# Strided 768 KB transfers issued from ScalarE's DMA queue in a two-part attention and long-convolution kernel

## The chip, the cores and the metric

The kernel runs on one core of one Trainium2 chip. Time is device time in microseconds (us) from one launch; the number that counts is the median of several runs. A profile of one execution comes with it: for each engine what ran when, what it waited for, and every packet of the DMA engines. TensorE (PE) multiplies matrices, VectorE (DVE), ScalarE (ACT) and GpSimd (POOL) do elementwise work, SyncE (SP) only issues DMAs. ScalarE may issue DMAs as well, from its own queue; in the page the queue of SyncE is q1 and that of ScalarE q10. The issues themselves are listed under SPq and ACTq, and are not counted as busy time.

## The reference

Two computations with no data in common write the left and the right half of one output (2048 x 1152, bfloat16).

Part A is attention with a compressive memory: 32 heads of 18 channels, 2048 positions in four segments of 512. Within a segment it is causal softmax attention; beside it, each segment reads a memory of all earlier segments; a gate per head mixes the two; a last product with `wo` follows.

```python
for s in range(N):
    logits = jnp.einsum('bhqd,bhkd->bhqk', qs, ks) * scale + mask
    a_dot = jnp.einsum('bhqk,bhkd->bhqd', _softmax(logits, axis=-1), vs)
    pq = phi(qs)
    a_mem = einsum(pq, M) / (einsum(pq, z) + 1e-06)
    outs.append(g * a_mem + (1.0 - g) * a_dot)
    pk = phi(ks)
    M, z = M + einsum(pk, vs), z + sum(pk)
return o @ wo
```

Part B is a gated long convolution over 576 channels: a four-tap convolution of `k`, times `v`, then a convolution with a filter of 2048 taps (`ssm_k`) by Fourier transforms, then a product with `q`.

```python
kv = k_shift * v
y = irfft(rfft(kv_pad) * rfft(kf_pad))[:S] + kv * ssm_D
return q * y
```

## The kernel before

**Tiling.** Part A goes over 4 segments and, in each, over 4 groups of heads `p`. The projections `proj_qk` and `proj_v` (L548, L607) read the transposed input `xT`; q and k go to a scratch tensor in DRAM (`store_rows`, L529) and come back with the channels of one head group on the right partitions (`load_heads`, L598, the tile `qk`). `scores` and `scores2` multiply them (L686), ScalarE takes the exponential into `PT` (L692), GpSimd masks (L698), `av` multiplies with V (L737). Numerators and denominators go through DRAM as well: `norm` stores `ou` (L752), `weights` fetches the denominators `cs` (L775) and stores their reciprocals (L790), `dense` fetches both as `nt` and `rt` (L811, L813), and `out_proj` multiplies with `wo` (L833) and stores (L839). `phik` fetches k once more, transposed by the DMA (L635); `load_x` does so with the next segment's input (L522).

Part B goes over three groups of 192 channels. `kv_prep` loads `k` and `v` transposed by the DMA (L1056), convolves four taps on TensorE (L1066), multiplies (L1070) and stores `kv_scratch` (L1074). `load_xs` (L1082) brings either the filter `ssm_k` or `kv_scratch` into the tile `xs` with 64 elements (128 bytes) to a piece: 6144 pieces, 768 KB. It is called six times, three for the filter and three for `kv_scratch`. `f1` (L1097) and `f2` (L1115) are the forward transform, `kloop` the products `Y` (L1152 to L1159), `inverse` (L1134) and `finish` (L1176, L1184) the way back. `last` loads `q_sb` (L1230), 768 KB in pieces of 384 bytes, and stores the result from the same tile (L1234). `begin` adds the small tensor `Dt` to `xs` (L1199) before `f1` can start; `Dt` and the taps `sk_bf` are loaded at L1042 to L1046.

**What sets the order.** The program is recorded first, as operations with their reads and writes. `Graph.plan` then lays them out one by one with its own cost for each: among the operations that can start within 0.3 us of the earliest on an engine it takes the one with the lowest priority number. An operation with alternatives (an eviction may run on VectorE or ScalarE) goes where the planned end is earlier, with a bias. `rank` gives priorities from the place in the recording, shifted by the table SHIFT; BIAS shifts the choice of engine, JOIN says where two TensorE operations are planned with their buffers together. Each engine then executes its list strictly in that order; so does each DMA queue. A DMA is an operation on the list of the engine that issues it; nearly all are on SyncE's, while ScalarE issues only the second half of the first input and most of `wk`.

In the planner a DMA occupies its issuer for a fixed time, then 16 modelled engines for a time that follows from number and size of its pieces; it lands a receipt time later. There are eight completion lanes that all DMAs of both issuers take in turn: a DMA waits until the one eight before it has landed.

**Where the planner puts fillers.** `gaps` finds planned holes of TensorE with much work around them, and puts matmuls on the identity there (L1359) that compute nothing of use.

**Names at the start.** `load0` is the first input and the weights `wq`, `wk` (L419, L420); `load1` is `wv` and the last columns of `wk`; `late_consts` with the label `late` copies `wo` within DRAM (L436), reloads it in another order (L441, L442), and loads `beta`. `tab` are the sine tables: two activations of 128 x 2048 (IS, IC) and smaller ones, on ScalarE, which needs another activation table for sines than for exponentials. `FI` is made from `FR` by a DMA (L991, L992).

Of the kernel before, what the change touches and what calls it, by code (L numbers as in the profile page):

```python
# [36 lines left out]
PEQ, ACTQ, DVEQ, POOLQ, SPQ = "PE", "ACT", "DVE", "POOL", "SP"  # L37
# [75 lines left out]
class Graph:  # L113
    SEM, DRAIN, SWITCH, MATE = 0.07, 0.2, 0.1, 0.03
    START, RECEIPT, LANES = 0.5, 1.3, 8
# [48 lines left out]
    def plan(self):  # L164
        free = {e: 0.0 for e in (PEQ, ACTQ, DVEQ, POOLQ, SPQ)}
        busy = dict(free)
        queue, lands = [0.0] * 16, [0.0] * self.LANES
# [3 lines left out]
        while left:  # L171
            best = {}
            for o in cand:
# [13 lines left out]
                for eng, us, emit in o.alts:  # L187
                    st = max(free[eng], t0)
                    for d in o.deps:
                        st = max(st, d.land + self.sem(d, eng))  # L190
                    best.setdefault(eng, []).append((st, o, us, emit, sl))
# [27 lines left out]
            if o.parts:  # L219

                e, one = st, us / len(o.parts)
                for n, share, k, ahead in o.parts:
                    e = max(e, lands[-self.LANES]) + one
                    for q in range(k):
                        queue[q] = max(queue[q], e - ahead + self.START) + share
                    lands.append(max(queue[0:k]) + self.RECEIPT)
                o.end, o.land = e, max(lands[-len(o.parts):])
# [113 lines left out]
class Part:  # L341
# [24 lines left out]
    def dma(self, parts, fn, r=(), w=(), us=0.4, ahead=0.0, by=(SPQ,)):  # L366

        nc = self.nc
        us *= len(parts)
        q = {SPQ: nc.sync, ACTQ: nc.scalar, POOLQ: nc.gpsimd}  # L370
        share = [(n, n * (8.0 + b / 27.0) * 1e-3 / k, k, ahead) for n, b, k in parts]
        return self.G.op([(e, us + (0.0 if e == SPQ else 0.15 * len(parts)), lambda e=e: fn(q[e])) for e in by], r, w, share)
# [528 lines left out]
class PartB(Part):  # L901
# [176 lines left out]
    def load_xs(self, src2d, g, keys):  # L1078
# [4 lines left out]
            "(c e) (a n) -> (e a) c n", e=4, a=KA)), r=keys, w=[xs])  # L1083
# [142 lines left out]
    def last(self, g):  # L1226
# [3 lines left out]
        self.dma([(2048, 384, 16)], lambda dq: dq.dma_start(out=q[:], in_=self.q_view[:, :, ch0:ch0 + GB]), w=[q])  # L1230
        for qq in range(0, QS, 8 * FD):
# [3 lines left out]
                 r=[(q, qq) for qq in range(0, QS, 8 * FD)])  # L1235
# [28 lines left out]
def rank(ops, a, b, shift):  # L1264
# [9 lines left out]
    'tab': 0.013, ('xs', 'in_B_ssm_k_dram', 0): 0.022, 'load0': -2, 'tr0': -1, ('qk', 0, 'first'): -1.5, ('qk', 0, 0): -1,  # L1274
    ('qk', 0, 5): -1, ('qk', 0, 6): -0.183, ('qk', 0, 4): -0.88, ('v', 0, 1): -0.168, ('x', 1): -0.088, ('qk', 1, 0): -0.572,
    ('sc', 0, 0, 0): 0.484, ('pk', 0): -0.042, ('sc', 0, 0, 1): 0.597, ('s2', 0, 1): -0.916, ('sc', 0, 1, 0): -0.046,
    ('sc', 0, 1, 1): 0.017, ('mem', 0): 0.054, ('s2', 0, 2): 0.007, ('no', 0, 1): 0.012, ('qk', 1, 1): -0.001,
    ('sc', 0, 2, 0): -0.002, ('av', 0, 2, 0): -0.222, ('s2', 0, 3): -0.013, ('qk', 1, 6): -0.152, ('sc', 0, 3, 1): 0.013,
    ('x', 2): -0.042, ('s2', 1, 0): -1.089, ('qk', 2, 0): 0.02, ('pk', 1): 0.555, ('v', 2, 0): 0.031, ('de', 0, 4): 0.327,
    ('sc', 1, 0, 1): -0.003, ('av', 1, 0, 0): -0.69, ('s2', 1, 1): -0.08, ('qk', 2, 5): -0.017, ('sc', 1, 1, 0): -0.011,  # L1280
    ('v', 2, 1): -0.009, ('sc', 1, 1, 1): -0.013, ('av', 1, 1, 0): -0.01, ('out', 0, 0): 0.015, ('qk', 2, 1): 0.02,
    ('sc', 1, 2, 0): -0.003, ('v', 2, 2): -0.006, ('s2', 1, 3): 0.006, ('qk', 2, 6): 0.001, ('av', 1, 3, 0): -0.302,
    ('no', 1, 3): -0.457, ('pk', 2): -0.017, ('de', 1, 0): 0.181, ('av', 2, 0, 1): -0.115, ('out', 1, 0): -0.327,
    ('v', 3, 2): 0.029, ('sc', 2, 2, 1): 0.014, ('out', 1, 1): 0.005, ('s2', 2, 3): 0.011, ('qk', 3, 6): 0.358,
    ('sc', 2, 3, 0): 0.003, ('v', 3, 3): 0.005, ('qk', 3, 4): -0.014, ('av', 2, 3, 1): 0.012, ('de', 2, 0): 1.659,
    ('de', 2, 3): -0.039, ('de', 2, 4): 0.397, ('sc', 3, 1, 0): 0.011, ('sc', 3, 1, 1): 0.01, ('s2', 3, 2): 0.029,
    ('sc', 3, 2, 0): 0.015, ('sc', 3, 2, 1): 0.029, ('out', 2, 2): 0.022, ('s2', 3, 3): 0.041, ('sc', 3, 3, 0): 0.04,
    ('sc', 3, 3, 1): 0.04, ('av', 3, 3, 0): 0.33, ('out', 2, 3): 0.03, ('de', 3, 0): 0.474, ('de', 3, 1): 0.369,
    ('de', 3, 2): -0.147, ('de', 3, 3): -0.427, ('de', 3, 4): -0.816, ('f1', 'A_h', 5, 8): -1.107, ('f1', 'A_h', 5, 16): -0.575,
    ('f1', 'A_h', 5, 24): 0.106, ('f1', 'A_h', 5, 32): 0.765, ('kv', 0, 9): -0.772, ('kv', 0, 1): 0.645, ('kv', 0, 3): -0.493,  # L1290
    ('kv', 1, 9): -0.286, ('kv', 1, 3): -0.791, ('xs', 'kv_scratch_69', 0): -1.316, ('f1', 'A_kv', 8, 0): -0.437,
    ('f1', 'A_kv', 8, 8): -1.241, ('f1', 'A_kv', 8, 16): -0.041, ('f1', 'A_kv', 8, 24): -0.654, ('f1', 'A_kv', 8, 32): -0.895,
    ('f1', 'A_kv', 8, 40): -0.691, ('row', 0, 0): -0.143, ('kv', 2, 0): -0.191, ('row', 0, 8): -1.15, ('y', 0, 8): -1.492,
    ('kv', 2, 1): -0.06, ('y', 0, 1): 1.118, ('row', 0, 9): 0.009, ('row', 0, 2): 0.003, ('inv', 8, 1): 0.005,
    ('kv', 2, 3): 0.004, ('row', 0, 10): 0.004, ('y', 0, 10): 0.184, ('inv', 8, 2): 0.021, ('f1', 'A_h', 10, 0): 0.032,
    ('row', 0, 11): 0.035, ('y', 0, 4): 0.464, ('f1', 'A_h', 10, 8): -0.018, ('row', 0, 12): 0.033,
    ('f1', 'A_h', 10, 16): 0.033, ('y', 0, 5): 0.438, ('inv', 8, 4): -0.118, ('row', 0, 13): 0.015, ('row', 0, 6): -0.192,
    ('f1', 'A_h', 10, 32): -0.381, ('row', 0, 14): 0.005, ('row', 0, 7): -0.109, ('row', 0, 15): 0.02,
    ('f1', 'A_kv', 11, 8): -0.007, ('fin', 8, 16): -0.325, ('fin', 8, 24): 0.02, ('f1', 'A_kv', 11, 24): 0.011,
    ('fin', 8, 32): 0.018, ('f1', 'A_kv', 11, 32): 0.018, ('f1', 'A_kv', 11, 40): -0.008, ('kv', 3, 1): -0.005,  # L1300
    ('row', 1, 1): -0.008, ('y', 1, 1): 0.115, ('kv', 3, 3): 0.04, ('row', 1, 10): 0.01, ('kv', 4, 9): 0.238,
    ('y', 1, 4): 0.131, ('inv', 11, 3): 0.01, ('kv', 4, 1): -0.668, ('kv', 4, 2): 0.096, ('y', 1, 13): -0.573,
    ('row', 1, 6): 0.011, ('inv', 11, 5): 0.003, ('f1', 'A_h', 14, 0): -0.486, ('row', 1, 14): 0.005,
    ('f1', 'A_h', 14, 8): -0.006, ('row', 1, 15): 0.002, ('f1', 'A_h', 14, 16): -0.018, ('f1', 'A_h', 14, 24): -0.022,
    ('f1', 'A_h', 14, 32): -0.025, ('f1', 'A_h', 14, 40): -0.062, ('f1', 'A_kv', 15, 0): -0.025, ('f1', 'A_kv', 15, 8): -0.029,
    ('f1', 'A_kv', 15, 16): -0.032, ('f1', 'A_kv', 15, 24): -0.008, ('f1', 'A_kv', 15, 32): 0.01, ('row', 2, 8): -0.001,
    ('row', 2, 9): 0.005, ('inv', 15, 1): 0.036, ('y', 2, 10): -0.075, ('y', 2, 3): 0.113, ('row', 2, 11): 0.019,
    ('row', 2, 4): 0.014, ('y', 2, 4): -0.471, ('inv', 15, 3): -0.508, ('row', 2, 12): -0.093, ('row', 2, 5): 0.344,
    ('y', 2, 5): 0.047, ('y', 2, 13): 0.644, ('row', 2, 6): 0.421, ('y', 2, 14): 0.452, ('row', 2, 7): -0.091,
    ('fin', 11, 0): 0.443, ('fin', 11, 16): -0.052, ('fin', 11, 24): -0.347, ('fin', 11, 40): -0.361, ('fin', 15, 24): -0.732,  # L1310
    ('fin', 15, 32): 0.277,
}
BIAS = {
    None: 0.3, 'tr0': 0, ('qk', 0, 0): 0, ('av', 0, 2, 1): 0, ('av', 1, 0, 0): 0.6, ('out', 0, 2): 1, ('av', 1, 2, 1): 1,
    ('v', 2, 3): -1.5, ('av', 1, 3, 0): 0, ('qk', 2, 4): -0.3, ('qk', 3, 0): -0.6, ('out', 1, 1): 3, ('out', 1, 3): -1.5,
    ('av', 3, 1, 0): 0.6, ('av', 3, 1, 1): -0.3, ('av', 3, 2, 0): 1.5, ('out', 2, 1): -1.5, ('out', 2, 2): -1.5,
    ('out', 3, 1): 0, ('f1', 'A_h', 5, 0): -0.6, ('y', 0, 0): 1, ('y', 0, 8): 1, ('y', 0, 1): 1, ('y', 0, 9): 1, ('y', 0, 2): 1,
    ('y', 0, 10): 1, ('y', 0, 3): 1, ('y', 0, 11): 1, ('row', 0, 4): -0.6, ('y', 0, 4): 3, ('y', 0, 12): 1, ('y', 0, 5): 1,
    ('y', 0, 13): 1, ('row', 0, 6): 1.5, ('y', 0, 6): -0.6, ('y', 0, 14): 1, ('row', 0, 7): -0.3, ('y', 0, 7): 1,
    ('f1', 'A_h', 10, 40): 3, ('y', 0, 15): 1, ('row', 1, 0): 0, ('y', 1, 0): 0, ('row', 1, 8): -1.5, ('y', 1, 8): 1,  # L1320
    ('y', 1, 1): 1, ('inv', 11, 0): 1.5, ('y', 1, 9): 1, ('y', 1, 2): 1, ('y', 1, 10): -0.3, ('y', 1, 3): 1, ('y', 1, 11): 1,
    ('y', 1, 4): 1, ('y', 1, 12): 1, ('y', 1, 5): 1, ('y', 1, 13): 1, ('row', 1, 6): -0.6, ('y', 1, 6): 1, ('y', 1, 7): 3,
# [70 lines left out]
```

## Time and profile before

| | |
|---|---|
| median of 13 runs | 353.01 us |
| lowest, highest | 349.58, 355.36 us |
| profiled execution | 352.95 us |
| its span, first to last instruction | 351.0 us |
| mean granted TensorE clock in it | 0.92 |

All times in what follows are inside the span of the profiled execution unless a run is named; 1.95 us lie around it. The page divides the span into 40 slices of 8.8 us; each digit is a busy share in tenths.

```profile
PE   4992999679885788779998888899897679977995
ACT  4571775767886389779796688776787876968850
DMA  8976969895476754591799668775977283252365
```

The fourth slice, from 26 to 35 us, is TensorE's emptiest. A timeline has one row for each instruction (or run of like ones): start, length, engine, line, operation, destination and source. SPq is an instruction of SyncE's queue: its length is the time for which it held the queue, and not the time of the transfer. In the chain of waits the work that ended last is followed backwards; "DMA x<-y" there is the time from issue to landing.

### The profile page before, as it was taken

What the parts mean: (1) busy time and instruction counts of PE and PEld (TensorE: products, weight loads), DVE (VectorE), ACT (ScalarE), POOL (GpSimd) and SP (SyncE); (2) the same over time, 40 slices, a digit from 0 to 9 for tenths busy, and PEclk for the clock granted to TensorE, in tenths of its full rate; (3) what the DMA queues carried; (4) which work ended last, traced back from release to release, by engine and by line L of the source; (5) the groups of instructions that cost most, each with busy time, mean ns of one, the idle gap of its engine ahead of it and who ended that gap; (6) DMA issues with size and microseconds to landing.
All of it is one profiled execution on the core that took longest, in us unless ns stands there. A gap on an engine that the chain in (4) does not pass through costs nothing.

```text
span 351.0 us, 9299 instructions
## 1 busy us (share of the span) xinstructions
PE 292.5 (83%) x3776; PEld 164.0 (47%) x3776; DVE 269.3 (77%) x390; ACT 248.0 (71%) x279; POOL 191.1 (54%) x262
## 2 busy tenths in 40 slices
PE   4992999679885788779998888899897679977995
PEld 3452545434453253556653344445454335544673
DVE  8953776576776289988976698898889795969993
ACT  4571775767886389779796688776787876968850
POOL 7723121167366359644246574795766368678710
PEclk9998899996999599999999699999999855989998
DMA  8976969895476754591799668775977283252365
GB/s 249 209 173 151 205 134 193 187 226 140 149 153 134 160 106 131 153 211 29 191 203 213 148 175 232 187 186 162 198 219 203 50 220 99 69 156 67 108 151 157
DMA packets 120369, 56.91 MB, mean 162 GB/s; under 512 B 93096, under 2 KB 113096, under 8 KB 120328
## 3 DMA queue, kind: packets, MB, share of 16 engines
q1 hardware_dynamic: 119448, 55.45, 65.6%
q10 hardware_dynamic: 880, 0.88, 0.8%
q8 instruction: 29, 0.48, 0.6%
q14 instruction: 12, 0.10, 0.1%
HBM read 25.66 MB, written 21.80 MB: 135 GB/s over the span
## 4 chain that ended last, share of the span: by engine, by line
PE 43%; DVE 17%; DMA 17%; ACT 9%; issue 7%; SPq 4%; POOL 2%; DVEq 0%; ACTq 0%; POOLq 0%
PE banks L548 8%; ACT PT L692 6%; DMA qk<-a_qk_scratch 6%; PE banks L833 5%; PE banks L686 5%; PE banks L1066 4%; PE banks L1134 3%; PE banks L607 3%; PE banks L737 3%; PE banks L1097 3%; DVE ou L363 3%; PE banks L1115 3%; DMA kv<-in_B_k_dram 2%; DMA rt<-a_r_scratch 2%; DVE nt L819 2%
## 5 line engine op out<-in xcount | busy, mean ns | idle before, releaser
L692 ACT ACTIVATE PT<-banks 128x1024 bf16<-128x1024 f32 x160 | 155.6, 1030 | 38.6 <-PE banks L686 30.9
L698 POOL TENSOR_SCALAR_AFFINE_SELECT PT<-PT 128x512 bf16<-128x512 bf16 (+1 forms) x112 | 83.3, 757 | 99.2 <-ACT PT L692 96.0
L686 PE MATMUL banks<-qk 18*128 18x512 bf16 (+3 forms) x512 | 54.1, 318 | 18.3 <-DMA qk<-a_qk_scratch 7.4
L548 PE MATMUL banks<-xT,wqk 128*128 128x512 bf16 x180 | 47.7, 407 | 2.2 <-DMA xT<-in_A_x_dram 0.7
L1152 POOL TENSOR_TENSOR Y<-HX 128x768 bf16<-128x768 bf16 x19 | 33.4, 1762 | 18.3 <-DVE HX L363 9.2
L686 PEld LDWEIGHTS <-qk 18*128 18x128 bf16 x512 | 16.2, 94 | 48.0 <-issue 31.6
L363 DVE CAST HX<-banks 128x768 bf16<-128x768 f32 x27 | 25.7, 956 | 11.1 <-PE banks L1115 9.4
L1158 POOL TENSOR_TENSOR Y<-Y 128x192 bf16<-128x192 bf16 x40 | 25.8, 645 | 10.8 <-DVE Y L1152 10.0
L363 DVE CAST A_kv<-banks 128x768 bf16<-128x768 f32 (+1 forms) x26 | 27.3, 1064 | 5.5 <-PE banks L1134 2.8
L1097 PE MATMUL banks<-W1bd,xs 128*64 128x128 bf16 x576 | 22.5, 231 | 10.0 <-DVE xs L1199 6.7
L363 DVE CAST ou<-banks 128x1024 bf16<-128x1024 f32 (+1 forms) x23 | 24.8, 1079 | 5.0 <-PE banks L737 3.2
L548 PEld LDWEIGHTS <-wqk 128*128 128x128 bf16 x180 | 16.9, 102 | 24.8 <-issue 10.4
L737 PE MATMUL banks<-PT,V 128*32 128x256 bf16 (+3 forms) x512 | 25.3, 318 | 2.4 <-ACT PT L692 0.8
L1097 PEld LDWEIGHTS <-xs 128*64 128x64 bf16 x576 | 19.0, 117 | 15.3 <-issue 7.9
L1159 POOL TENSOR_TENSOR Y<-Y 128x192 bf16<-128x192 bf16 x40 | 26.0, 650 | 0.0
L833 PE MATMUL banks<-wo_sb,o_sb 128*128 128x288 bf16 x160 | 24.6, 312 | 1.6 <-DVE o_sb L820 1.0
L1066 PE MATMUL banks<-kv,dg 128*128 128x512 bf16 x80 | 20.1, 387 | 5.1 <-DMA kv<-in_B_k_dram 4.4
L1134 PE MATMUL banks<-Y,IC 64*128 64x192 bf16 x192 | 22.2, 260 | 1.7 <-DVE V L363 0.6
L607 PE MATMUL banks<-wv,xT 128*128 128x288 bf16 x160 | 23.1, 297 | 0.4 <-ACT HX L364 0.4
L364 ACT CAST HX<-banks 128x768 bf16<-128x768 f32 x21 | 16.8, 805 | 5.6 <-PE banks L1115 5.3
L819 DVE TENSOR_TENSOR nt<-nt,rt 128x1024 bf16<-128x1024 bf16 (+1 forms) x15 | 18.4, 1228 | 3.1 <-DMA rt<-a_r_scratch 3.1
L833 PEld LDWEIGHTS <-o_sb 128*128 128x128 bf16 x160 | 16.4, 106 | 8.9 <-issue 1.8
(146 smaller groups left out, 535.9 us busy)
## 6 DMA issues: line engine op xcount, KB each, us to landing
a_o_scratch<-ou SPq DMA_DIRECT2D x12, 512.0 KB
qk<-a_qk_scratch SPq DMA_DIRECT2D x48, 108.0 KB
a_qk_scratch<-q SPq DMA_DIRECT2D x32, 128.0 KB
nt<-a_o_scratch SPq DMA_DIRECT2D x12, 256.0 KB
rt<-a_r_scratch SPq DMA_DIRECT2D x12, 256.0 KB
xs<-in_B_ssm_k_dram SPq DMA_DIRECT2D x3, 768.0 KB
xs<-kv_scratch SPq DMA_DIRECT2D x3, 768.0 KB
q_sb<-in_B_q_dram SPq DMA_DIRECT2D x3, 768.0 KB
```

The source lines that it names most:

```text
L363: return self.G.op([(DVEQ, dve_us(n, 0.53 if bf else 1.042), lambda: nc.vector.tensor_copy(out=out(), in_=in_())), (ACTQ, act_us(n), lambd ...
L548: nc.tensor.matmul(pq[:], lhsT=self.wqk[:, t, 128 * m:128 * m + P], rhs=xT[:, t, :], start=(t == 0), stop=(t == 4))
L607: nc.tensor.matmul(out, lhsT=xT[:, t, P * tt:P * tt + P], rhs=self.wv[:, t, 288 * h:288 * h + 288], start=(t == 0), stop=(t == 4))
L686: nc.tensor.matmul(ps[:, j - j0, off:off + n], lhsT=qk[r, 2 + u, P * kt:P * kt + P], rhs=qk[r, u, P * kt:L], start=True, stop=True, tile_p ...
L692: self.act(act_us(512 * SE), lambda a=a, ps=ps, j=j, j0=j0: nc.scalar.activation(out=a(dst), in_=ps[:, j - j0:j - j0 + SE, :], func=ACT.Ex ...
L698: self.pool(0.2 + n * 0.13, lambda: nc.gpsimd.affine_select(out=ap(), in_=ap(), compare_op=ALU.is_ge, fill=0.0, base=0, pattern=[[0, n], [ ...
L737: nc.tensor.matmul(po[32 * j:32 * j + 32, 0, P * kt:L], lhsT=V[:, kt, 19 * h:19 * h + 32], rhs=rhs, start=(kt == 0), stop=(kt == 3), tile_ ...
L833: nc.tensor.matmul(ps[:, i, 0:288], lhsT=o[:, t, P * qt:P * qt + P], rhs=self.wo[:, t, 288 * h:288 * h + 288], start=(t == 0), stop=(t == ...
L1066: self.pe(pe_us(*[512] * 4 * w), lambda c=c, ps=ps: [nc.tensor.matmul(ps[:, 512 * h:512 * h + 512], lhsT=dg[:, i, :], rhs=t[:, 0, KPAD + 5 ...
L1097: nc.tensor.matmul(ps[64 * h:64 * h + 64, u, :], lhsT=xs[:, c0 + u, :], rhs=self.W1[:, h].rearrange("p e k -> p (e k)"), start=True, stop= ...
L1134: nc.tensor.matmul(ap(b)[:, o, :], lhsT=tab[q, r + 8 * h, :], rhs=Ys[h][q, n, :], start=(h == n == 0), stop=(h == n == 1), tile_position=( ...
L1152: eng.tensor_tensor(out=Y[:].rearrange("p (x h) c -> p x h c", x=2), in0=HX[:, 1, :].rearrange("p (x c) -> p x c", x=2).unsqueeze(2).to_br ...
```

## The change

It has five parts.

1. `load_xs` (all six loads of `xs`) and the load of `q_sb` in `last` are issued by ScalarE (`by=(ACTQ,)`). The stores of the result may be issued by either; the planner chose ScalarE for the last of the three and SyncE for two.
2. The planner has a set of 16 modelled engines for each of the two queues. A transfer on one is lengthened by what the other still has to do, up to its own time, and lengthens the other by as much.
3. It knows a limited room: after a transfer, the next DMA of the same queue may start only when all but the last 80 pieces of each ring (RING) are done.
4. No transfer is planned to run before 2.2 us (FIRST), and bytes are costed at 23 instead of 27 a nanosecond.
5. SHIFT, BIAS and JOIN are replaced throughout. Among other things `late` is shifted ahead (-0.349), so that the copy of `wo` comes directly behind the first weights, and `wv` (`load1`) after it.

```diff
-    START, RECEIPT, LANES = 0.5, 1.3, 8
+    START, RECEIPT, LANES, FIRST, RING = 0.5, 1.3, 8, 2.2, 80
...
-        queue, lands = [0.0] * 16, [0.0] * self.LANES
+        queue, lands = {e: [self.FIRST] * 16 for e in (SPQ, ACTQ)}, [0.0] * self.LANES
+        open_ = {SPQ: 0.0, ACTQ: 0.0}
...
-                    st = max(free[eng], t0)
+                    st = max(free[eng], t0, open_[eng] if o.parts else 0.0)
...
+                mine, other = (queue[x] for x in ((SPQ, ACTQ) if eng == SPQ else (ACTQ, SPQ)))
                 for n, share, k, ahead in o.parts:
-                    e = max(e, lands[-self.LANES]) + one
+                    e = max(e, lands[-self.LANES], open_[eng]) + one
                     for q in range(k):
-                        queue[q] = max(queue[q], e - ahead + self.START) + share
-                    lands.append(max(queue[0:k]) + self.RECEIPT)
+                        t = max(mine[q], e - ahead + self.START)
+                        both = min(share, max(0.0, other[q] - t))
+                        mine[q] = t + share + both
+                        if both:
+                            other[q] += both
+                    lands.append(max(mine[0:k]) + self.RECEIPT)
+                    open_[eng] = max(mine[0:k]) - self.RING * k * share / n
...
-        share = [(n, n * (8.0 + b / 27.0) * 1e-3 / k, k, ahead) for n, b, k in parts]
+        share = [(n, n * (8.0 + b / 23.0) * 1e-3 / k, k, ahead) for n, b, k in parts]
...
-            "(c e) (a n) -> (e a) c n", e=4, a=KA)), r=keys, w=[xs])
+            "(c e) (a n) -> (e a) c n", e=4, a=KA)), r=keys, w=[xs], by=(ACTQ,))
...
-        self.dma([(2048, 384, 16)], lambda dq: dq.dma_start(out=q[:], in_=self.q_view[:, :, ch0:ch0 + GB]), w=[q])
+        self.dma([(2048, 384, 16)], lambda dq: dq.dma_start(out=q[:], in_=self.q_view[:, :, ch0:ch0 + GB]), w=[q], by=(ACTQ,))
...
-                 r=[(q, qq) for qq in range(0, QS, 8 * FD)])
+                 r=[(q, qq) for qq in range(0, QS, 8 * FD)], by=(ACTQ, SPQ))
...
 SHIFT = {
-    'tab': 0.013, ('xs', 'in_B_ssm_k_dram', 0): 0.022, 'load0': -2, 'tr0': -1, ('qk', 0, 'first'): -1.5, ('qk', 0, 0): -1,
+    'tab': 0.023, ('xs', 'in_B_ssm_k_dram', 0): 0.024, 'load0': -2, 'tr0': -1, 'load1': 0.026, ('qk', 0, 'first'): -1.5,
+    ('qk', 0, 0): -1, ('qk', 0, 5): -1.105, ('qk', 0, 1): 0.036, ('qk', 0, 4): -0.132, 'late': -0.349, ('v', 0, 0): -0.337,
...
```

In the order that comes out, SyncE issues ten DMAs fewer. ScalarE issues 13 instead of 3, and has five activation table loads instead of two. The first `xs` is ScalarE's fourth DMA; the first `xs` from `kv_scratch` stands ahead of an exponential of `q`, a V eviction and four of the PT exponentials.

## The prediction

> **What bounds the kernel now.** I read the page first: no engine is full, so the order and the waits decide.
>
> ```profile
> PE 292.5 (83%) x3776; PEld 164.0 (47%) x3776; DVE 269.3 (77%) x390; ACT 248.0 (71%) x279; POOL 191.1 (54%) x262
> ...
> q1 hardware_dynamic: 119448, 55.45, 65.6%
> q10 hardware_dynamic: 880, 0.88, 0.8%
> ...
> PE 43%; DVE 17%; DMA 17%; ACT 9%; issue 7%; SPq 4%; POOL 2%; DVEq 0%; ACTq 0%; POOLq 0%
> ```
>
> Nearly all packets go through one queue (q1, SyncE's); ScalarE's (q10) has 880. In the chain of waits DMA and SyncE's queue hold 21% of 351 us, some 74 us. So I looked at SyncE's timeline, at what follows each `xs` or `q_sb` transfer (768 KB in elements of 128 or 384 bytes); times are start and length in us.
>
> ```profile
> 10.84 0.53 SPq L1082 DMA_DIRECT2D xs<-in_B_ssm_k_dram  x1
> 11.42 6.72 SPq L1045 DMA_DIRECT2D sk_bf<-in_B_shift_k_dram  x1
> ...
> 27.28 0.62 SPq L1042 DMA_DIRECT2D Dt<-in_B_ssm_D_dram  x1
> ...
> 56.59 0.53 SPq L1082 DMA_DIRECT2D xs<-kv_scratch  x1
> 57.21 3.83 SPq L529 DMA_DIRECT2D a_qk_scratch<-q  x1
> ```
>
> ```profile
> 244.43 0.56 SPq L1082 DMA_DIRECT2D xs<-kv_scratch  x1
> 245.04 6.36 SPq L1230 DMA_DIRECT2D q_sb<-in_B_q_dram  x1
> 251.49 2.59 SPq L598 DMA_DIRECT2D qk<-a_qk_scratch  x4
> ```
>
> The long transfer itself is handed over in half a microsecond; the next instruction of the queue then sits for 4 to 6 us. A plain issue takes about 0.5 us (the L529 median, 506 ns), so the excess is 6.2 us at 11.42, 3.3 at 57.21, 4.1 at 73.89, 2.2 at 100.04 (a transpose of 3.44 us, against 1.25 for its sisters), 6.0 at 245.04, and 2.5 in single issues around these: 24 us of SyncE held. The 5.76 us of a transpose at 175.56 follows none of them, and I leave it out.
>
> How much of this reaches the end the chain and the waits show:
>
> ```profile
> 27.28 5.44 DMA Dt<-in_B_ssm_D_dram
> ...
> 112.82 4.91 DMA qk<-a_qk_scratch
> ...
> 253.75 5.51 DMA qk<-a_qk_scratch
> ```
>
> ```profile
> PE banks L1097 <- DVE xs L1199: 6.7, 1, 6.7
> ```
>
> ```profile
> 27.00:34.00 7.00, 0.72 (x14) 0.72 (x16) 2.20 (x4) 0.76 (x2) 2.43 (x3) 0.84 0.51 117
> ```
>
> TensorE works 0.72 us of the seven from 27 to 34: it waits for the add of `Dt`, a load of 1.1 KB whose issue stood behind the stall. The two loads of `qk` on the chain take about 5 us, where others on it take 2.5 to 2.9 (at 62.74 and 92.45).
>
> **What the Trainium skill says.** "DMA: Bandwidth & Descriptors", section "Queues, rings and completion order": SP and ACT each own one ring on each of the same 16 DMA engines, and an engine goes round its rings packet by packet. So a long transfer in ScalarE's ring holds up no ring of SyncE's and shares only the engines. Same page, "Issuing engines are not separate DMA queues": a second issuer saves only issue time, no bandwidth. The trace agrees that the saving is issue time (24 us held) and has no case of a full ring on ScalarE. Against it, "Perfetto Trace Analysis", "DMA Instruction — HWDGE (DVE, Sync)" calls the descriptor generator a shared block that is locked by its user; were ScalarE's transfer to hold it for 5 us, SyncE would stall as now. In the first 2.5 us both queues issue side by side at 0.46 to 0.58 us each, so no lock shows there, but those transfers are short.
>
> **The change part by part.** The changed program's order was compared engine by engine; sums are against the profiled execution (351.0 us span, 352.95 us run; the median of the runs is 353.01).
>
> *Nine loads and one store leave SyncE for ScalarE.* SyncE loses ten issues (5 us) and the stalls. Place by place:
> - Start, 6.2 us. ScalarE now issues the first `xs` fourth, at about 2.5 us by its present issues. But in the new order `Dt` is still SyncE's 23rd, behind the `wo` copies (648 KB) and their reload, five `a_qk_scratch` stores, `FI`, `wv` and the tail of `wk`. With `x`, `wq`, `wk` and `wo`, 2.47 MB at the 253 GB/s of the first ten us is 9.8 us, some 2 of `xs` packets between (13.3 ns each, read from the packets) and 2 to land make 13 to 14; then 5 reloads (3.5 us) and 11 issues at 0.5: `Dt` at about 23, against 27.28. 4 us earlier. `wv` comes as late as 24, however, so TensorE lacks the three heads of `V` it did before 27 (3.7 us), filled in part by score tiles moved forward. I count 2 (0 to 5).
> - At 57.21: 3.3 us held, TensorE idle only 0.85 just there and 2.4 by 72: 1.5 (0 to 3.3).
> - At 73.89: what waited is the first `dense` (o_sb, 6.1 us of VectorE's), with other work beside it: 0 to 1, taken 0.
> - At 100.04: 2.2 held, then the chain goes through `qk` at 112.82 and TensorE waits 4.9 us in four pieces: 1.5 (0 to 4).
> - At 245.04: 6.9 held, but TensorE, VectorE and ScalarE are busy 12.98, 12.85 and 12.22 us of the fifteen from 245, so the cover is good: 2 (0 to 6.9).
> - At 262 to 272: `a_o_scratch<-ou` takes 5.13 us on the chain behind the second `q_sb`; the four waits for such transfers at L775 come to 10.9, 2.7 each: 1 (0 to 2).
> Sum 8.0, of at most 22.
>
> *What ScalarE pays.* Ten issues at 0.5 us (its own three take 0.49 to 0.57): 5 us. ScalarE is idle 29% of the span, and 9% of the chain is its own: I charge 30%, 1.5 (0.5 to 5). Three more activation table loads (5 against 2, because exponentials of the first score tile now stand between sines) at 1283 ns: 3.8 us, one ahead of everything and two at 15 to 27 us, where ScalarE is busy 10.7 of 17: 0.5 on the path (0 to 2.6).
>
> *New waits on ScalarE.* The three loads `xs<-kv_scratch` wait for the landing of the `kv` store, now with ScalarE's in-order stream behind them. The first stands ahead of an exponential of `q`, a `V` copy and four PT exponentials, for which TensorE's score banks and GpSimd's masks wait; its store is SyncE's 43rd, behind five `xT` transposes (1.26 each). The trace shows no such wait on ScalarE. Bounds: nothing, where the store has landed; 5 us, where SyncE does four transposes in between. ScalarE is idle 5.3 of the 12 us from 45 to 57, which hides most. I take 1 in all (0 to 6). The others read inputs and wait for a semaphore of a DMA eight back: nothing.
>
> *Moved copies and tables.* The new SHIFT, BIAS and JOIN change who evicts: ScalarE gets seven more HX (805 ns) and four A_h (1018), and gives seven q (592), four ou (1016), four oA and three V (640); VectorE the reverse. That is -2 us on ScalarE, -1 on VectorE, +1 on GpSimd, five more filler matmuls (0.38) in idle gaps: nothing (-3 to +3, because the whole list is drawn anew).
>
> *Constants, the planner.* RING, FIRST and the slower byte rate only change the order above.
>
> Sum: -8.0 + 1.5 + 0.5 + 1.0 = -5.0 us. 351.0 becomes 346.0; with the 1.95 us around the span 347.95, against a median 0.06 above the profiled run: **348 us**.
>
> **Rivals.**
> 1. *The stalls go, and the next wait has the time.* TensorE 83%, VectorE 77%: the list is dense, and 74 us of DMA on the chain are mostly round trips that remain. For: from 245 the engines were busy anyway. Against: the seven empty microseconds at 27. Gain at most the 2 of the start, less ScalarE's 2: 353.
> 2. *ScalarE is held by its loads, slower.* One mechanism: at the first `xs<-kv_scratch` near 55 us ScalarE stands until the store has landed, and score tiles and masks stand with it. With three waits of 6 us, 4 of each covered by ScalarE's idle time, 6 us; half of the 8 us of gains lost to the rest of the list, -4; issues and tables, 2: 353 + 4 = 357. It turns at waits of 4.7 us each, and is slower beyond what can be told at 5.3. For: SyncE has the transposes ahead. Against: SyncE is unburdened by then, and ScalarE has slack.
> 3. *It does not do what it says.* The generator is shared, SyncE still stalls, and ScalarE has 2 us more to do on the path: 355.
>
> **How the numbers follow.** Forecast 0.62, first rival 0.13, second 0.16, third 0.09. A measurement here tells about 0.5% (1.8 us) from no change. Forecast, own range 340 to 351: faster. First rival: same, with a few hundredths to either side. Second: slower. Third: slower by most of it. Together faster 0.64, same 0.14, slower 0.22. The low end takes 13 of the 22 us of gains at once; the high end reaches into the second rival: 340 to 357.
>
> **What would show it.** Right: no SyncE issue of 4 to 7 us behind an `xs` or `q_sb`; q10 with about 46000 packets (36864 of `xs`, 8192 of `q_sb`, its own 880); TensorE's hole at 27 to 34 shorter by 2 or more; `qk` loads on the chain near 3 us. Wrong: SyncE issues as long as before (third rival); ScalarE idle for several microseconds ahead of an `xs` issue, with TensorE waiting on PT just after (second); stalls gone, span equal (first). The size is wrong if the start loses more to the late `wv` than `Dt` gains.

## The result, and the profile after

| | before | after |
|---|---|---|
| median, timed together | 353.29 us (48 runs) | 351.58 us (11 runs, 346.23 to 359.3) |
| ratio after to before | | 0.9868 [0.9819, 0.9916] |
| profiled execution, span | 352.95, 351.0 us | 355.89, 354.2 us |
| mean granted TensorE clock in it | 0.920 | 0.917 |

The ratios here and below leave out, for both kernels, the runs that lie over 1.5% above the kernel's fastest, which the medians do not. In a second set of runs (kernel before: 351.65 us) the changed kernel had a median of 351.0 us and 0.9902 [0.987, 0.9934]. So by the ratios it is 1.0 to 1.3% faster, 3.4 to 4.7 us; by the medians of all runs only 0.2 to 0.5%. The profiled execution lies near the upper end of the kernel's own runs: where its time went can be read from it, but not the total. A second profile of the same kernel (first experiment) has a span of 351.6 us.

The page after, lines as quoted of before:

```profile
PE 295.7 (83%) x3781; PEld 163.6 (46%) x3781; DVE 276.3 (78%) x391; ACT 250.9 (71%) x276; POOL 193.7 (55%) x267
...
q1 hardware_dynamic: 74232, 47.59, 53.3%
q10 hardware_dynamic: 46096, 8.75, 13.1%
...
PE 43%; DVE 25%; DMA 14%; ACT 6%; issue 5%; SPq 3%; POOL 3%; DVEq 0%; ACTq 0%; POOLq 0%
```

The transfers have moved: q10 has 46096 packets. On the chain of waits DMA fell from 17% to 14%, and VectorE rose from 17% to 25%. ScalarE's DMA issues in the timeline (start, length):

```profile
58.05 0.41 ACTq L1090 DMA_DIRECT2D xs<-kv_scratch  x1
68.89 0.39 ACTq L1090 DMA_DIRECT2D xs<-in_B_ssm_k_dram  x1
...
256.31 0.37 ACTq L1090 DMA_DIRECT2D xs<-kv_scratch  x1
274.87 0.38 ACTq L1238 DMA_DIRECT2D q_sb<-in_B_q_dram  x1
```

They take 0.4 us each; no issue of ScalarE's lasts as long as SyncE's did behind a long transfer. The time SyncE spends in DMA issues, summed over its timeline, fell from 204.8 to 179.5 us. So the stalls of 4 to 7 us in an issue right behind an `xs` or `q_sb` on the same queue are gone from SyncE. What it shows instead (a row with x4 is four issues and the time between them):

```profile
61.04 7.44 SPq L606 DMA_DIRECT2D qk<-a_qk_scratch  x4
...
70.17 4.56 SPq L1064 DMA_TRANSPOSE kv<-in_B_k_dram  x1
74.77 3.80 SPq L1064 DMA_TRANSPOSE kv<-in_B_v_dram  x1
```

In the waits of SyncE (total, times, longest) the first of these rows has a name that the kernel before did not have:

```profile
SPq L606 <- DMA xs<-kv_scratch: 5.7, 1, 5.7
```

The kernel's eight completion lanes are shared by both issuers; the eighth DMA after the long transfer, on SyncE, waits until that has landed. In the chain of waits:

```profile
27.57 5.55 DMA Dt<-in_B_ssm_D_dram
...
70.17 8.76 DMA kv<-in_B_k_dram
```

`Dt` is issued no earlier than before (27.57 against 27.28). Yet the hole from 27 to 34 us is filled, TensorE working 4.51 us of it instead of 0.72:

```profile
27.00:34.00 7.00, 4.51 (x27) 2.06 (x25) 2.71 (x5) 6.95 (x7) 6.88 (x4) 1.00 0.61 156
```

The work in it is score tiles, V, projections and a few fillers that the new order has moved there. And the load of `kv` at 70 us takes 8.76 us from issue to landing. Here the question starts: is the gain the queue's, or the order's?

### The profile page after: what moved, and what is told of

Read it like the earlier page. It is cut to its first block, busy times and chain, and to the rows that moved or that the text cites. A ratio compares the mean times of both kernels' runs of the same rounds, so it can differ in the third digit from the quotient of the medians.

```text
span 354.2 us, 9316 instructions
## 1 busy us (share of the span) xinstructions
PE 295.7 (83%) x3781; PEld 163.6 (46%) x3781; DVE 276.3 (78%) x391; ACT 250.9 (71%) x276; POOL 193.7 (55%) x267
## 3 DMA queue, kind: packets, MB, share of 16 engines
q10 hardware_dynamic: 46096, 8.75, 13.1%
## 4 chain that ended last, share of the span: by engine, by line
PE 43%; DVE 25%; DMA 14%; ACT 6%; issue 5%; SPq 3%; POOL 3%; DVEq 0%; ACTq 0%; POOLq 0%
PE banks L556 7%; PE banks L1074 5%; PE banks L694 5%; PE banks L841 5%; DMA rt<-a_r_scratch 5%; PE banks L1105 4%; PE banks L615 4%; DVE ou L371 4%; PE banks L745 4%; DMA qk<-a_qk_scratch 3%; ACT PT L700 3%; DVE HX L371 3%; PE banks L1123 3%; DMA kv<-in_B_k_dram 2%; PE banks L589 2%
## 5 line engine op out<-in xcount | busy, mean ns | idle before, releaser
L694 PE MATMUL banks<-qk 18*128 18x256 bf16 (+3 forms) x512 | 53.0, 318 | 13.9 <-DVE HX L371 3.1
L556 PE MATMUL banks<-xT,wqk 128*128 128x512 bf16 x180 | 44.8, 390 | 6.0 <-DVE q L371 3.7
L1160 POOL TENSOR_TENSOR Y<-HX 128x768 bf16<-128x768 bf16 x17 | 30.8, 1813 | 14.6 <-DVE HX L371 7.6
L371 DVE CAST ou<-banks 128x1024 bf16<-128x1024 f32 (+1 forms) x27 | 28.6, 1061 | 12.2 <-PE banks L748 8.2
L372 ACT CAST HX<-banks 128x768 bf16<-128x768 f32 x28 | 22.1, 813 | 12.6 <-PE banks L1123 11.8
L1160 DVE TENSOR_TENSOR Y<-HX 128x768 bf16<-128x768 bf16 x31 | 24.3, 793 | 5.2 <-ACT HX L372 4.3
L1074 PE MATMUL banks<-kv,dg 128*128 128x512 bf16 x80 | 22.7, 424 | 3.2 <-DMA kv<-in_B_k_dram 3.2
L371 DVE CAST q<-banks 128x512 bf16<-128x512 f32 x26 | 17.8, 688 | 9.5 <-PE banks L556 7.8
L841 PE MATMUL banks<-wo_sb,o_sb 128*128 128x288 bf16 x160 | 22.1, 286 | 1.1 <-DVE o_sb L828 0.8
L372 ACT CAST A_kv<-banks 128x768 bf16<-128x768 f32 (+1 forms) x17 | 15.0, 889 | 10.2 <-PE banks L1142 7.7
```

Of the source, the lines that this page charges most:

```text
L371: return self.G.op([(DVEQ, dve_us(n, 0.53 if bf else 1.042), lambda: nc.vector.tensor_copy(out=out(), in_=in_())), (ACTQ, act_us(n), lambd ...
L372: (ACTQ, act_us(n), lambda: nc.scalar.copy(out=out(), in_=in_()))], r, w)
L556: nc.tensor.matmul(pq[:], lhsT=self.wqk[:, t, 128 * m:128 * m + P], rhs=xT[:, t, :], start=(t == 0), stop=(t == 4))
L694: nc.tensor.matmul(ps[:, j - j0, off:off + n], lhsT=qk[r, 2 + u, P * kt:P * kt + P], rhs=qk[r, u, P * kt:L], start=True, stop=True, tile_p ...
L841: nc.tensor.matmul(ps[:, i, 0:288], lhsT=o[:, t, P * qt:P * qt + P], rhs=self.wo[:, t, 288 * h:288 * h + 288], start=(t == 0), stop=(t == ...
L1074: self.pe(pe_us(*[512] * 4 * w), lambda c=c, ps=ps: [nc.tensor.matmul(ps[:, 512 * h:512 * h + 512], lhsT=dg[:, i, :], rhs=t[:, 0, KPAD + 5 ...
```

## The experiments

All were timed in five rounds beside the kernel before (median 351.65 us for e0 to e3, 353.57 for e4 to e7, 353.52 for e8 to e11).

**Queue against order.** Two kernels fill the square of two orders and two queues, beside the changed kernel once more.

> The changed kernel once more, beside the next three, for a second profile of it. Theory A (the gain comes from ScalarE's queue, which takes the long transfers out of SyncE's way) and theory B (it comes from the list drawn anew by SHIFT, BIAS and JOIN) expect the same of it: ratio 0.982 to 0.992 to the kernel before, span near 346 us. TensorE's first product of the heads should again start near 10.9 us and the load of Dt be issued near 27.5 us if those two places belong to the order and not to one execution.

Measured: 351.0 us, 0.9902 [0.987, 0.9934].

The changed order, long transfers back on SyncE:

```diff
         q = {SPQ: nc.sync, ACTQ: nc.scalar, POOLQ: nc.gpsimd}
+        if ACTQ in by and self.G.label != "load0":
+            q[ACTQ] = nc.sync
```

> The changed kernel's order of all engines, but its ten long transfers are issued by SyncE again, each at its place in the order. Theory A: SyncE's issues behind an xs or q_sb last 4 to 7 us again, some 24 us in all, and the ratio rises from 0.987 to between 1.00 and 1.03 (the 8 us of gains that the prediction counted, and ScalarE gets back 5 us of issues). Theory B: the stalls come back but the ratio stays within 0.5% of the changed kernel's.

Measured: 341.83 us, 0.9737 [0.9696, 0.9777].

The old order with the long transfers on ScalarE's queue; the same `on=nc.scalar` stands at `q_sb` and at the last store:

```diff
-            "(c e) (a n) -> (e a) c n", e=4, a=KA)), r=keys, w=[xs])
+            "(c e) (a n) -> (e a) c n", e=4, a=KA)), r=keys, w=[xs], on=nc.scalar)
```

> The kernel before, its order of all engines kept, but with nine long loads and the last store issued by ScalarE at their places in the order. Theory A: ratio 0.98 to 0.99, the stalls of 3 to 6 us behind xs and q_sb are gone from SyncE. Theory B: 0.995 to 1.01, since the list was drawn without these waits on ScalarE. The rival of the prediction in which ScalarE is held by the loads: above 1.005, with ScalarE idle for several us ahead of an xs from kv_scratch.

Measured: 360.35 us, 1.0168 [1.0108, 1.0228].

| | long transfers on SyncE | on ScalarE |
|---|---|---|
| order of before | 1 | 1.0168 |
| new order | 0.9737 | 0.9902 |

The queue costs 1.7% (5.9 us) in both orders, and the new order brings 2.6% (9.2 us). The change is faster in spite of its first part. The medians of all runs, put in place of the ratios, give 1.0247 for e2, 0.9721 for e1 and 0.9982 for e0: the same signs, and a larger price of the queue. Neither theory had expected e1 to be faster than e0; e2 lies where the prediction's second rival put it, but for another reason, as follows. The equal price in the two orders need not have one cause.

**Where the queue costs, old order.** In e2 ScalarE issues two long transfers in succession. Its timeline:

```profile
246.73 0.37 ACTq L1082 DMA_DIRECT2D xs<-kv_scratch  x1
247.13 6.79 ACTq L1230 DMA_DIRECT2D q_sb<-in_B_q_dram  x1
253.97 1.02 ACT L692 ACTIVATE PT<-banks 128x1024 bf16<-128x1024 f32 x1 [6.74 <-DMA xs<-kv_scratch]
```

and TensorE's, just after (the bracket is its idle time and what ended it):

```profile
255.04 0.61 PE L686 MATMUL banks<-qk 18*128 18x512 bf16 x2 [6.24 <-ACT PT L692]
```

It is the stall of before (6.36 us at 245.04) on another engine. While SyncE had it, TensorE's longest wait between 236 and 262 us was 1.3 us. ScalarE has the exponential behind it, which the scores' PSUM banks wait for. The test puts this one `q_sb` back on SyncE:

```diff
-w=[q], on=nc.scalar)
+w=[q], on=nc.scalar if g != 1 else None)
```

> The kernel before in its own order with its long transfers on ScalarE's queue (which was 1.7% slower than before), except the second q_sb, which goes back to SyncE. In the trace of that kernel ScalarE's issue of it at 247 us lasted 6.8 us behind an xs in the same ring, with exponentials behind it in its list, and TensorE stood 6.2 us. Theory, the stall was moved to a worse engine: the 6 to 7 us go with this one transfer, ratio 0.995 to 1.001. Rival, the cost is in sharing and lanes all along the list: 1.010 to 1.018.

Measured: 351.08 us, 0.9969 [0.9928, 1.001], as the theory said. The issue on SyncE, and TensorE's waits for the exponential between 236 and 262 us:

```profile
243.05 0.59 SPq L1230 DMA_DIRECT2D q_sb<-in_B_q_dram  x1
```

```profile
PE banks L686 <- ACT PT L692: 0.4, 1, 0.4
```

One transfer of ten is worth 2.0% (7 us), the whole cost of the queue in this order. The other nine on ScalarE give 0.3%, which can't be told from nothing, although SyncE's time in issues is 178.2 us, against 204.8 before. Two things did not cost anything that can be measured either: SyncE waits 10.5 and 4.9 us at lanes for long transfers of ScalarE's, and the `xs` of 243 us, now beside `q_sb`, takes 12.2 us from first to last packet instead of 5.8. Whether the old stalls had been covered, or these waits took their place, is not separated.

**Where the queue costs, new order.** Here the planner keeps the long transfers of one queue apart (RING), and no issue of ScalarE's stalls. e0 and e1 have the same order on every engine but for the issues, so like instructions of VectorE can be compared one by one. The table has the median lag behind e1 in stretches of 10 us of e1's time (our own working from the traces, also for later experiments). `after` is the same kernel as e0, and e10 the same as e1:

```
from us     60    70    80    90   110   150   210   220   250   290   320
e0         1.4   2.1   6.4   6.4   6.0   5.8   5.7   8.0   8.4  12.1  12.2
after      1.3   1.9   6.4   6.4   6.2   6.4   7.0   7.1   9.8  14.5  14.7
e4         1.5   1.6   3.1   3.9   3.2   3.6   4.5   4.8   5.3   7.2   7.3
e8         3.6   4.0   4.2   4.2   3.6   4.0   2.4   0.9   1.8   5.1   5.9
e10        1.4   1.7   3.2   4.0   1.7   1.3   1.8   1.8   1.8   2.3   2.2
e11       -3.3  -2.9  -2.9  -2.9  -5.8  -4.9  -4.2  -3.3  -3.3   1.6   2.0
```

These are single executions: e10 lies up to 4 us behind e1, though it is the same kernel, and the 12.2 us of e0 at the end are twice what the ratios give for the queue (5.9). e0 loses 4.3 us between 70 and 80 (`after` 4.5, e10 1.5), 2.3 at 220, and 3.7 between 250 and 290. The second is not in `after`. The third is (4.7), but e11, with all long transfers on SyncE, loses 4.9 there too, so it is not shown to be the queue's. Only the first is followed here.

At this place, e1 (SyncE, then TensorE):

```profile
68.06 2.11 SPq L1066 DMA_TRANSPOSE kv<-in_B_k_dram  x1
70.23 0.58 SPq L1092 DMA_DIRECT2D xs<-in_B_ssm_k_dram  x1
70.86 6.38 SPq L1066 DMA_TRANSPOSE kv<-in_B_v_dram  x1
```

```profile
74.13 1.03 PE L1076 MATMUL banks<-kv,dg 128*128 128x512 bf16 x4 [0.24 <-ACT PT L702]
```

and SyncE and TensorE in e0:

```profile
70.23 4.45 SPq L1064 DMA_TRANSPOSE kv<-in_B_k_dram  x1
```

```profile
78.89 1.89 PE L1074 MATMUL banks<-kv,dg 128*128 128x512 bf16 x4 [2.86 <-DMA kv<-in_B_k_dram]
```

In e1 SyncE even stalls for 6.4 us, with nobody waiting: the urgent transpose of `k` stood ahead of the long transfer in the same queue. In e0 it runs beside it. By the packets, the long transfer of 58 us takes 7.5 us from first to last in e0 and 4.3 in e1. That of 69 us runs from 70.2 to 78.1 in e0, and the transpose's 2048 packets from 73.9 to 78.0 among its own; in e1 they run from 69.4 to 72.7, and 1959 of them come ahead of the long transfer's first. The Trainium skill, "DMA: Bandwidth & Descriptors", section "Queues, rings and completion order", says that an engine goes round its rings packet by packet. The trace agrees by these numbers, and this is the price: with a second queue the urgent transfer no longer goes ahead of the long one.

The second figure is the clock: the same four matmuls take 1.89 us after the hole and 1.03 without it. "TensorE: Matmul & The Clock Gate", section "Part 1: The HAM clock gate", states half rate after an idle window of about 3.4 us. In e0's trace the clock is at half for 6.8 us from 77.55, but TensorE was not idle in the 3.41 us before that: it worked 1.28 us of them, and its hole was 1.5 us old. So here less than the stated idle time was enough (the stretch; its second number is TensorE's work):

```profile
74.14:77.55 3.41, 1.28 (x24) 0.84 (x20) 2.73 (x4) 3.27 (x4) 0.49 (x1) 1.00 1.36 166
```

Three experiments work at this place. e4 puts only the transfers of 58 and 69 us back on SyncE:

```diff
+        if ACTQ in by and str(self.G.label[1])[0:2] + str(self.G.label[-1]) in ("kv0", "in1"):
+            q[ACTQ] = nc.sync
```

> The changed kernel, with only two of its ten long transfers back on SyncE: the first xs from kv_scratch and the second xs from ssm_k (those issued at 58 and 69 us). Put back all together, the ten brought 9 us (351.0 to 341.8 us). Theory, one place: half of this was lost right there, where kv transposes come late beside the long transfers and TensorE stands 2.9 us and then runs at half clock. Then two of ten bring half or more: ratio to the kernel before 0.978 to 0.982 (344 to 345.5 us with the kernel before at 351.7), and TensorE's wait for kv is gone. Rival, the cost is spread evenly over the ten: two tenths of it, 0.986 to 0.988 (347 us or more in these terms).

Measured: 347.61 us, 0.9843 [0.9784, 0.9902]. TensorE:

```profile
75.73 1.03 PE L1076 MATMUL banks<-kv,dg 128*128 128x512 bf16 x3 [0.24 <-ACT PT L702]
```

The wait is gone; up to 90 us e4 lies where e10 does, and at the end its lag is 4.9 us smaller than e0's. The ratio lies between the two forecasts, and its interval reaches both.

e8 leaves everything on ScalarE, and moves the issue of 69 us down ScalarE's list, behind the kv transposes:

```diff
     def run(self):
         self.plan()
+        self.redo()
         self.emit()
...
+    def redo(self):
+        x = [x for x in self.log if x[2] == ACTQ and x[3].parts and x[3].label == ("xs", "in_B_ssm_k_dram", 1)][0]
+        self.later(x, self.at(ACTQ, ("row", 0, 1)))
```

(`at` finds an entry of the planned list, `later` puts one directly ahead of another.)

> The changed kernel, all long transfers on ScalarE's queue as in it, but the second xs from ssm_k (issued at 69 us, first needed after 100 us) is moved some 8 us down ScalarE's list, behind the issues of the kv transposes that SyncE makes at 70 and 75 us. Theory, sharing: at this place it was the transfer's packets among the kv transposes' that made TensorE stand 2.9 us and lag 4 us; with the transposes ahead the transfer may stay on ScalarE. Then the wait of TensorE for kv is below 1 us, the lag between 70 and 85 us gone, and the ratio to the kernel before is 0.976 to 0.982, as with the pair on SyncE. Rival, the shared completion lanes and ScalarE's list decide and not the sharing: no change, 0.986 to 0.992.

Measured: 347.41 us, 0.9893 [0.9815, 0.9972]. SyncE's issue, its wait at the lane, and TensorE:

```profile
72.05 2.16 SPq L1076 DMA_TRANSPOSE kv<-in_B_k_dram  x1
```

```profile
SPq L618 <- DMA xs<-kv_scratch: 5.6, 1, 5.6
```

```profile
78.16 1.02 PE L1086 MATMUL banks<-kv,dg 128*128 128x512 bf16 x3 [0.24 <-ACT PT L712]
```

The transpose's issue takes 2.16 us instead of 4.45, TensorE waits 0.24 instead of 2.86, and the lag grows by 0.2 between 70 and 80 instead of 4.3, although SyncE still waits at the lane (5.6 us). This execution was already 3.6 us late at 60, so the fair measure is from the issue of the transpose to TensorE's product with it: 6.1 us in e8 as in e1, 8.7 in e0. So at this place it was the sharing, and not the lane. In the whole time it does not show: the ratio is no better than e0's (0.9902) and lies where the rival put it, while the interval just reaches the theory. Neither e4 nor e8 shows, then, that this place makes up the 5.9 us.

e6 keeps the changed kernel's queues and puts 52 matmuls on the identity into five holes:

```diff
             last = e
+        for i, n in {260: 12, 406: 9, 868: 15, 933: 10, 1180: 6}.items():
+            out[id(self.log[i][3])] = n, self.log[i][0]
         return out
```

> The changed kernel, long transfers on ScalarE as in it, with 52 matmuls on the identity that compute nothing, in five holes of TensorE of its trace: 12 ahead of the product with kv at 78 us, 9 at 111, 15 at 209, 10 at 224, 6 at 278. Theory, the clock multiplies the cost: at each of these holes the granted clock fell to half for 7 to 20 us, and that is most of the 9 us between the two queues. Then the mean clock goes from 0.91 to 0.95 or more, TensorE's busy time without the fillers falls by 5 us or more, and the ratio is 0.974 to 0.982. Rival, the holes themselves cost and the clock only follows: clock up, time the same within 1.5 us, 0.985 to 0.992. Slower (over 0.995) if the fillers stand in the way of work that was ready.

Measured: 355.89 us, 1.0101 [1.0036, 1.0165]: slower, the last of the three forecasts. The mean clock is 0.950 against 0.911 in the profiled executions, and 0.948 against 0.935 over the runs behind the ratios. TensorE:

```profile
77.08 2.75 PE L1370 MATMUL banks<-ident 128*128 128x512 bf16 x12 [0.24 <-ACT PT L702]
79.66 1.03 PE L1076 MATMUL banks<-kv,dg 128*128 128x512 bf16 x3
...
209.58 4.96 PE L1370 MATMUL banks<-ident 128*128 128x512 bf16 x15 [3.74 <-DVE q L373]
```

At 78 the fillers do what was hoped: the product with `kv` runs at full rate, and between 70 and 80 us, counted as in the table, this kernel loses 2.2 us where e0 loses 4.3. At 209 they do harm: they themselves waited 3.74 us for VectorE's eviction of `q` from their PSUM bank, and then kept TensorE for 5 us while work was ready. e7 does the same to e1, with 29 fillers in three holes (`{418: 8, 868: 15, 1210: 6}`):

> The changed kernel's order with all ten long transfers on SyncE, and 29 such fillers in its own holes: 8 ahead of the scores at 106 us, 15 at 203, 6 at 276. Clock theory: its half-rate stretches of 7, 10 and 3 us shrink, some 2 to 3 us less: ratio 0.965 to 0.969. Rival: the same as without, 0.972 to 0.976.

Measured: 347.38 us, 0.9812 [0.9747, 0.9877]. This is above both forecasts and above e1 (0.9737), though the intervals overlap: no gain, and perhaps a loss. It shows the same two cases:

```profile
104.84 1.90 PE L1372 MATMUL banks<-ident 128*128 128x512 bf16 x8
...
200.46 6.20 PE L1372 MATMUL banks<-ident 128*128 128x512 bf16 x15 [3.48 <-DVE q L373]
```

By VectorE's instructions it is some 4 us ahead of e1 at 120, and level with it at 210, after the second. Both kernels therefore don't decide what the clock is worth in all. e6 shows that a higher mean clock can go with a slower kernel.

**The start.** In the new order `late` stands early, and with it arithmetic for the gates (small VectorE operations) ahead of the first eviction of `xT`. VectorE and TensorE in e1:

```profile
4.68 1.70 DVE L481 TENSOR_SCALAR gbits<-row_a 128x2 int32<-128x2 int32 x2
...
10.11 1.02 DVE L371 COPY xT<-banks 128x1024 bf16<-128x1024 bf16 x2
```

```profile
10.85 5.52 PE L591 MATMUL banks<-xT,wqk 128*32 128x512 bf16 x65 [2.71 <-DVE xT L371]
```

e3 moves that arithmetic back behind the start, with the queues of the change; e5 and e11 are e1 with the same edit:

```diff
+    def redo(self):
+        end = self.at(DVEQ, "late", 1)
+        self.later(self.at(POOLQ, "late"), end)
+        self.later(self.at(DVEQ, "late", 0), end)
```

> The changed kernel with the index arithmetic of the late constants (GpSimd's iotas and memsets at L465 to L467, VectorE's ten small operations at L473 to L483) moved behind the first evictions, to just ahead of the rest of the gate's arithmetic at L489. If it is what delays the first product of the heads from 8.7 to 10.9 us, that product starts at 8.7 us again, FR and the rows behind it come 2 to 4 us earlier, and the ratio falls by 0.4 to 0.8% below the changed kernel's. If the start has slack there (the load of Dt is issued at 27.6 us either way, and f1 waits for it), the first product starts earlier and the time stays within 0.3%.

Measured: 346.96 us, 0.9871 [0.9827, 0.9915]. TensorE's first product starts at 7.99 us instead of 10.85, but the ratio is only 0.3% below e0's and the intervals overlap: what was forecast if the start has slack. (The medians differ by more, 346.96 against 351.0.)

> The changed kernel's order, all ten long transfers on SyncE, and besides the gate arithmetic of late (GpSimd's iotas, VectorE's index steps) moved behind the start. Theory, the start decides: the first product of the heads is 3 to 4 us earlier, and that reaches the end as its median did with ScalarE's queue (351.0 to 347.0): ratio 0.961 to 0.966. Rival, what was gained at the start is lost by 100 us, as the ratio of fast runs said of it (0.9902 against 0.9871): 0.971 to 0.975.

Measured: 342.61 us, 0.963 [0.9551, 0.9709], as forecast if the start decides.

To compare it with e1 side by side, both were timed once more.

> The changed kernel's order with all ten long transfers on SyncE, once more, to stand beside the next on the same chip: 0.970 to 0.978.

Measured: 344.54 us, 0.9753 [0.9642, 0.9865].

> The same with the gate arithmetic of late moved behind the start. If the 3 to 5 us gained at the start reach the end: 0.960 to 0.968, and its interval below that of the run without. If other waits take them: 0.970 to 0.978, the same as without.

Measured: 341.37 us, 0.9718 [0.9648, 0.9789]. TensorE in e11:

```profile
7.98 4.50 PE L604 MATMUL banks<-xT,wqk 128*32 128x512 bf16 x80 [0.33 <-DVE xT L384]
```

The first product comes 2.9 us earlier and runs at full rate. The last row of the table shows what becomes of it: about 3 to 6 us ahead until 250, then nothing left by 290. This time the ratio lies where the rival put it. The intervals of e10 and e11 overlap, and the medians differ by 3.2 us in its favour; whether it gains is not settled. Both kernels are faster than before and after, by 2.5 to 2.8% against before.

## Why the prediction was right, and what in it was wrong

The sign and the size were right: 5.0 us forecast, 3.4 to 4.7 measured. The reason was not, and so this was luck: two errors of opposite sign. The sum had -5 from the queue (-8 gained, +3 paid) and 0 from the order; measured were about +6 and -9.

- *"Nine loads and one store leave SyncE for ScalarE", -8.0.* This is the step that failed. The stalls left SyncE as described, but the time did not follow: in the old order the nine transfers other than the second `q_sb` give -0.3% [-0.7, +0.1], so next to nothing of the stalls taken from SyncE with them reached the end. They were the most visible waits of SyncE's timeline, but not what the kernel waited for. e1 has the long issues back (6.38 us at 70.86) and is the faster kernel.
- *The 6.9 us held at 245, counted at 2 because the engines were busy.* The cover was rightly seen; the other half of the question, what the same stall costs on its new engine, was not asked. In the old order it came back whole (6.79 us on ScalarE, 7 us of the time). In the new order the two transfers are issued 18.6 us apart (256.31 and 274.87), and ScalarE has no such stall.
- *The start, -2 by an earlier `Dt`.* `Dt` was issued at 27.57 instead of 23: SyncE waited for the `q` stores until 20.17 and for the copy of `wo`. The hole closed all the same by moved work, with either queue (4.51 us in e1 too), so this belongs to the order.
- *"What ScalarE pays", +1.5 and +0.5.* The issues took 0.4 us, one 0.8. The table loads were five, as forecast; their price was not tested apart.
- *"New waits on ScalarE", +1.0.* The wait for the `kv` store that the prediction feared is there at the first of the three. ScalarE has finished its work at 55.71, the store lands at 57.95, and only then does the issue follow:

```profile
53.77 1.94 ACT L372 CAST A_h<-banks 128x1024 bf16<-128x1024 f32 x2
58.05 0.41 ACTq L1090 DMA_DIRECT2D xs<-kv_scratch  x1
58.55 1.06 ACT L570 ACTIVATE e<-q 128x1024 bf16<-128x1024 bf16 x1 [2.84 <-DVE q L371]
```

This costs 0.3 us at most, because the next operation had to wait for VectorE's `q` until 58.27 anyway. At 103 and 256 us there is no such wait. Two other costs stood in the sum nowhere: the sharing with an urgent transfer (4.3 us at 70 to 80 in e0) and the wait of SyncE for the long transfer's lane (5.7 us, which did no harm at this place in e8). The first lies in what the prediction itself had quoted from the skill: it drew from it "holds up no ring of SyncE's", and took "shares only the engines" to cost nothing.
- *"Moved copies and tables", nothing, -3 to +3.* This term failed as well: it measured -9.2 us, three times its bound. A list that is drawn anew as a whole gives no reason to expect nothing. Where the order gains was looked for, not tested apart. With the queue held equal (SyncE), VectorE worked 31.7 of the fifty microseconds from 70 to 120 before and 41.4 in e1; by our own count of TensorE's columns without the fillers, e1 is about 3 us behind before at 70 and about 7 ahead at 120.
- *Rivals.* The third (it does not do what it says) is refuted: SyncE's stalls are gone, and in e2, while ScalarE stood in the issue of 247.13 for 6.79 us, SyncE issued five DMAs in 0.30 to 0.39 us each, so no generator that both share was locked all that time. The second (ScalarE is held by its loads) was seen in e2, by the issue right behind a long transfer and not by the `kv` store; in the changed kernel the store's wait is there, and covered. The first (stalls go, the next wait has the time) describes the queue part best, and was too mild in the new order, where the queue costs time.

What stays open: where the queue costs its 5.9 us in the new order beyond the place at 70 to 80 us, and how much even of that place reaches the end; the loss from 250 to 290 us, which kernels with either queue have; how much of the queue's cost is the half-rate clock; and which of the many moves of the new order bring its 9.2 us.

## What to carry to other kernels

A stall that stands out in a queue is worth what waits behind it: before moving it, ask who stands behind it on the new engine, and what it will share the DMA engines with. One queue with the urgent transfer ahead of the long one can beat two queues, even where the issuer stalls behind the long one; where nothing urgent runs beside it, sharing cost nothing that could be measured here. And when a change also redraws the order, build the two mixed kernels first: the square of order and queue cost two runs here, and told what no reading of the trace did.

## What the runs showed of the hardware, unexpected

- The stall behind a long transfer with small pieces goes with the queue and not with SyncE: `q_sb` behind `xs` held SyncE for 6.36 us and ScalarE for 6.79, and the other queue's issues went on beside it.
- Small VectorE operations on 2 to 32 columns mostly took about 0.95 us each at 2.5 to 7.4 us into the run (one took 0.16), and 0.15 us from 8 to 9.3, in the same trace (e1). GpSimd works until 7.9 us there and then stands until 10.7; whether that is the cause was not tried.
- Filler matmuls need a free PSUM bank to be of use: fifteen of them waited 3.5 to 3.7 us for an eviction, and then ran for 5 to 6 us, at 0.33 to 0.41 us each; where twelve ran without such a wait, it was 0.23 us each.
- TensorE's clock fell to half, for 6.8 us, although TensorE had worked 1.28 of the 3.41 us before (e0, 74.14 to 77.55).
